# Ten additions of weight halves on GpSimd in place of VectorE, in a recurrence and mixture-of-experts kernel

## The chip, the cores and the metric

The kernel runs on one core of one Trainium2 chip. The metric is the device time of one execution in microseconds (us); lower is better. Engines are called by their short names: PE is TensorE (matmuls; PEld is its weight load), DVE is VectorE, ACT is ScalarE, POOL is GpSimd, SP issues most of the DMAs.

## What is computed

Two blocks follow each other, all in float32. The first is a recurrence over 768 time steps, for 4 batches of 8 heads of width 40:

```python
for t in range(S):
    y[:, :, t] = einsum('bhd,bhde->bhe', rt, state)
    Sa = einsum('bhde,bhe->bhd', state, at)
    state_decay = state * wt[:, :, None, :] - einsum('bhd,bhe->bhde', Sa, bt)
    state = state_decay + einsum('bhd,bhe->bhde', vt, kt)
```

Its output, laid out as x of 3072 tokens by 320, goes into a mixture of four experts, all of which see every token (w1 is 320x1024 and w2 is 1024x320 for each expert):

```python
p = domain_probs / (domain_probs.sum(-1, keepdims=True) + 1e-09)
for e in range(E):
    h = maximum(x @ w1[e], 0.0)
    out += p[:, e:e + 1] * (h @ w2[e])
```

## The kernel before

**Units.** The recurrence is cut into chunks of 64 time steps. A unit is one chunk of two batches; there are 24, numbered 0 to 23, and two of them make up one chunk of all four batches. Within a unit the recurrence becomes matmuls on 64x64 blocks and one triangular solve. `within` prepares a unit (decays G, the turned operands AT, RT and VT, the scaled n_tok and k_tok, score matrices F, ET and VC). `substitute` does the solve: copies of F's diagonal blocks into `blocks` (two on DVE, two on ACT), one large transpose into M on DVE, a few products on DVE, and then 16 rounds of a product (L585) and two additions (L598) of small tiles Z. For units 0 and 1 the rounds run on DVE, for all others on POOL. `merge` turns Z into Qc and QTc (DVE) and QT (four copies on POOL, L617), and joins the two halves of the solve through the matmuls pY and pQ. `step` is the part that depends on the state: RH (DVE), SN (ACT), psat, SaT and SX, pxr, RS, pdy, then the output Y and the new state.

**The mixture.** Work of the experts is a list of pieces, `todo`, from which `gap` takes one or two at four places in every unit, so that PE has work while the recurrence waits. For units 0 and 1 it is done plainly (`mixture_of_unit`). From the second chunk on, `mixture_of_chunk` does the second matmul for two units together by a Strassen-like scheme on halves: of the hidden values (`add_h`, L903, on DVE) and of the second weights (`add_weights`, L869). The latter makes, for each expert, three new tiles in `sums` and overwrites two halves of `w2_sb` in place: five operations of 128x640, made once, before the first `down_1` of their expert; expert 2's are read first at unit 5's `gap(1)`, expert 3's in the same unit's `gap(3)`. The tile of `sums` of the last expert is before that the place of the constant `pick`, which the matmuls pxT of units 0 to 3 read; the other three hold pieces of the first weights up to unit 1's mixture.

**Where the sums stand.** `sums_at` says how many of them are issued at which `gap`: one at each from unit 2's `gap(1)` to unit 4's `gap(2)`, which is experts 0 and 1, and then 2, 3, 2 and 3 at the four gaps from unit 4's `gap(3)` to unit 5's `gap(2)`, which is experts 2 and 3.

**Order.** A planner orders each engine's instructions by priority and its own estimate of when their inputs are there. `tc.keep_in_program_order` pins an instruction behind the one written just before it on the same engine. Matmuls of the main loop are pinned, as are the sums, the solve's first operations and the copies on POOL. The loop over u runs the step of unit u, the merge and the first part of the step of unit u + 1, and the preparation and the solve of unit u + 2. At the head of an iteration POOL has just been given the solve of unit u + 1; the QT copies of unit u + 1 and the solve of unit u + 2 follow. Units below `EARLY` (5) have a different order of these parts from later ones.

Of the kernel before, what the change touches and what calls it, by code (L numbers as in the profile page):

```python
# [15 lines left out]
def kernel(  # L16
# [38 lines left out]
    nc = tc.nc  # L55

    B, H, S, D = r.shape
    E, DM, F = moe_w1.shape
# [26 lines left out]
    def big(name):  # L85
# [6 lines left out]
        out=ident[:], in_=ident[:], pattern=[[1, P]], compare_op=ALU.is_equal, fill=0.0,  # L92
# [5 lines left out]
    for t, n, op in ((upf, L, ALU.is_gt), (diagf, Q, ALU.is_equal)):  # L98
        nc.vector.memset(t[:], 1.0)
        for q in range(P // n):  # L100
            o = slice(q * n, (q + 1) * n)
            nc.gpsimd.affine_select(
                out=t[o], in_=t[o], pattern=[[1, n]], compare_op=op, fill=0.0, base=0, channel_multiplier=-1,
# [83 lines left out]
    def sooner(wanted):  # L187
        return tc.high_priority(offset=SOONER) if wanted else nullcontext()
# [3 lines left out]
    def begin(u):  # L192
        q = Unit()
        q.u, q.c, q.bp = u, u // (B // 2), u % (B // 2)
        q.b = [2 * q.bp, 2 * q.bp + 1]
        q.start, q.end = q.c == 0, q.c == NC - 1
        q.apart = u >= EARLY + 2
        q.n = {}
        units.append(q)
        return q  # L200

    def load(q, names):
        for x in names:
            q.n[x] = t = sb.tile([P, H, D], FP32, name=f"nat{x}", tag=f"nat{x}", bufs=2 if x in "WV" else 1)
            for i, bb in enumerate(q.b):
                nc.sync.dma_start(
                    out=t[i * L:(i + 1) * L], in_=srcs[x][bb, :, q.c * L:(q.c + 1) * L, :].rearrange("h t e -> t h e"),
                )
# [30 lines left out]
    def go(moves, eng=None):  # L239
        for move in moves:  # L240
            move(eng or nc.sync)
# [362 lines left out]
    def merge(q):  # L604


        Qc = sb.tile([P, H, Q], FP32, name="Qc", tag="q", bufs=2)
        QTc = sb.tile([P, H, Q], FP32, name="QTc", tag="q", bufs=2)
        tc.keep_in_program_order(nc.vector.transpose(out=dealt(Qc[:]), in_=q.Z))
        tc.keep_in_program_order(  # L610
            nc.vector.transpose(  # L611
                out=QTc[:].rearrange("p h r -> p (h r)"), in_=Qc[:].rearrange("p h c -> p (h c)"),
            )
        )
        q.QT = QTs()
        for i in range(P // Q):
            ins = nc.gpsimd.tensor_copy(out=q.QT[quarter(i), :, quarter(i % 2)], in_=QTc[quarter(i)])  # L617
            tc.keep_in_program_order(ins)
        yield

        def two_heads(name, lhsT, rhs, to):
            p = big(name)
            for n in range(NJ):
                for r in range(2):
                    matmul(
                        out=p[half(r), n * 2 * Q:(n + 1) * 2 * Q], lhsT=lhsT[half(r), 2 * n:2 * n + 2, :],
                        rhs=rhs[half(r), 2 * n:2 * n + 2, :], start=True, stop=True,
                    )
            for r in range(2):
                for y in range(2):  # L630
                    src = p[quarter(2 * r + y), 0:H * Q].rearrange("p (n two t) -> p n two t", two=2, t=Q)[:, :, y, :]
                    with sooner(name == "pY"):
                        nc.scalar.copy(out=of_slot(to[quarter(2 * r)], y), in_=src)

        Y = Ys()
        two_heads("pY", q.below, QTc, Y)
        yield

        two_heads("pQ", Qc, Y, q.QT[:, :, quarter(1)])
        yield  # L640
# [212 lines left out]
    def of_w2(e, q, x):  # L853
        return w2_sb[e][:, q * HF:(q + 1) * HF, x * HD:(x + 1) * HD]

    def of_sums(e, n):
        return sums[e][:, n * HF * HD:(n + 1) * HF * HD].rearrange("p (f d) -> p f d", d=HD)

    def add_weights(e):

        b = {(q, x): of_w2(e, q, x) for q in range(2) for x in range(2)}
        for to, x, y, op in (
            (of_sums(e, 0), b[0, 0], b[1, 1], ALU.add),
            (of_sums(e, 1), b[0, 0], b[0, 1], ALU.add),
            (of_sums(e, 2), b[1, 0], b[1, 1], ALU.add),
            (b[0, 1], b[0, 1], b[1, 1], ALU.subtract),
            (b[1, 0], b[1, 0], b[0, 0], ALU.subtract),
        ):
            tc.keep_in_program_order(nc.vector.tensor_tensor(out=to, in0=x, in1=y, op=op))  # L869
            yield  # L870

    def mixture_of_chunk(qs, xT):
# [98 lines left out]
    def begin_later(n):  # L971
        for move in later[:n]:
            tc.keep_in_program_order(move(nc.sync))
        del later[:n]

    def mix(n):

        for piece in todo[:n]:
            ready = stores[:]
            del stores[:]  # L980
            piece()
            for begin_store in ready:
                begin_store()
            begin_later(3 if n > 1 else 6)
        del todo[:n]

    def lead():
        if todo and hasattr(todo[0], "lead"):
            todo[0].lead()

    def run(gen, n=99):
        if gen is None:
            return
        for _ in range(n):
            if next(gen, gen) is gen:
                break
# [3 lines left out]
    def begin_step(u):  # L1000
        q = units[u]
        if q.bp == 0:
            chunks_x[q.c] = sb.tile([P, 3, 2 * P], FP32, name="xT", tag="xT", bufs=2)
        q.xT = chunks_x[q.c][:, :, q.bp * P:(q.bp + 1) * P]
        return step(q, q.xT)
# [95 lines left out]
    sparse = range(4 * 1, 4 * 4 + 2)  # L1101

    sums_at = {4 * 2 + n: 1 for n in range(1, 11)}
    sums_at.update({4 * 4 + 3: 2, 4 * 5 + 0: 3, 4 * 5 + 1: 2, 4 * 5 + 2: 3})
    sum_ops = (None for e in range(E) for _ in add_weights(e))
    for u in range(1, NU):
        in_order[0] = True
        q = units[u]
        m = s_next = w = w_next = iter(())
        if u + 1 < NU:  # L1110
            m, s_next = merge(units[u + 1]), begin_step(u + 1)
            w_next = ws[u + 1]
        if u + 2 < NU:
            w = ws[u + 2]

        def gap(n, pieces=None):
            at = 4 * u + n
            run(sum_ops, sums_at.get(at, 0))
            mix((1 if at in sparse else 2) if pieces is None else pieces)

        early = u < EARLY
        if early:
            begin_later(len(later))
        ahead = u + 3 < NU and u in range(EARLY, EARLY + 3)
        if ahead:
            go(load_raw(begin(u + 3), "W"))
        if early:
            lead()
        run(w_next, 99 if early else 1)
        run(s, 1)  # L1130
        gap(0)


        if early:
            run(s, 1)
        run(w, 1)
        if not early:
            run(w_next)
            run(s)

        if early:
            run(w, 1)
            gap(1, 2 if u + 1 == EARLY else None)
            run(s)
        if u == 1:
            mixture_of_unit(q)
        elif q.bp:
            mixture_of_chunk(units[u - 1:u + 1], chunks_x[q.c])
        if not early:
            begin_later(len(later))  # L1150
            run(w, 1)
            lead()
            todo[:2] = todo[1::-1]
            gap(1)
            run(m, 1)

        if u + 3 < NU:
            go(load_raw(units[u + 3] if ahead else begin(u + 3), "A" if ahead else "WA"))
            load(units[u + 3], "WBKV")
            later.extend(load_raw(units[u + 3], "VR"))  # L1160
        run(w, 2)

        soon = u in (2, 3, 4)
        if soon:
            run(w, 1)
        if early:
            run(m, 1)
        else:
            run(m, 1)
            run(s_next, 1)  # L1170
            lead()
            run(m, 1)
            if u + 3 < NU:
                ws.append(within(units[u + 3]))
                run(ws[u + 3], 1)
        if soon:
            substitute(units[u + 2], nc.gpsimd)
        gap(2)

        if u == 1:  # L1180
            run(s_next, 1)
            run(m, 1)
        if not soon:
            run(w, 1)
        if not soon and u + 2 < NU:
            with sooner(not early):
                substitute(units[u + 2], nc.gpsimd)
        if not early:
            lead()
            run(s_next, 1)  # L1190
        if early:
            run(w, 1)
        if early:
            ws.append(within(units[u + 3]))
            run(ws[u + 3], 1)
            if u > 1:
                run(m, 1)
                run(s_next, 1)
            run(m)
            gap(3, 1)  # L1200
            run(s_next, 1)
        else:
            begin_later(len(later))
            gap(3)
        s = s_next
# [31 lines left out]
```

## Time and profile before

| | us |
|---|---|
| median of 3 runs | 1095.37 (1095.02 to 1099.68) |
| the profiled execution's own time | 1096.91 |
| its span in the profile | 1095.2 |
| PE busy | 1068.1 (98%) |
| DVE busy | 759.0 (69%) |
| POOL busy | 490.3 (45%) |
| the 20 sums on DVE (L869): 12 into sums, 8 in place | 10.4 and 6.8 |
| mean of one of them | 0.88 and 0.87 |

The profile is one execution, taken by the hardware profiler. In a group of instructions the columns are line, engine, operation, tiles written and read, shape and count, then busy time and mean duration in ns. In a timeline they are the start and the duration in us and what ran; in brackets stands the idle time of the engine just before, and what ended it. Most operations on PE go through a helper, so they all have line L76; there the names of the tiles tell them apart. Durations on POOL are rougher than those of other engines. The solves of units 4, 5, 6 and 7 on POOL begin at 149.5, 179.8, 212.2 and 264.1 us.

### The profile page before, as it was taken

The numbers are of one execution on the slowest core, as the hardware profiler recorded it, in microseconds if no ns is written. First come the engines' busy times: TensorE is split into PE (matmuls) and PEld (weight loads), VectorE is DVE, ScalarE is ACT, GpSimd is POOL, SyncE is SP. The second block draws the span as 40 slices with busy tenths as digits, with TensorE's granted clock in tenths as the row PEclk, the third lists the DMA queues.
The fourth block names the chain that finished last, engine by engine and source line by source line (L and its number), as shares of the span: only waits on it lengthen the run. The fifth ranks groups of instructions, "written<-read, shape, count | busy, mean of one in ns | idle before, by whom it ended". The sixth has DMA issues, their size and how long they took to land.

```text
span 1095.2 us, 38536 instructions
## 1 busy us (share of the span) xinstructions
PE 1068.1 (98%) x16102; PEld 959.0 (88%) x16102; DVE 759.0 (69%) x1551; ACT 353.4 (32%) x956; POOL 490.3 (45%) x1274
## 2 busy tenths in 40 slices
PE   7798999999999999999999999999999999999998
PEld 6677788889998999999999999989999999998887
DVE  7676569887776777767768768767777676544343
ACT  2432444234223333333233242343333332221110
POOL 5206577763472562653643634735625536420000
PEclk8799999999999999999999999999999999999999
DMA  7876545434444463454454454444543532322320
GB/s 118 236 231 142 131 91 131 107 77 108 120 119 105 110 144 97 103 146 97 100 133 105 106 122 106 115 99 105 131 103 85 149 89 60 99 71 79 107 75 13
DMA packets 268869, 122.19 MB, mean 112 GB/s; under 512 B 213736, under 2 KB 242072, under 8 KB 268696
## 3 DMA queue, kind: packets, MB, share of 16 engines
q1 hardware_dynamic: 265416, 119.12, 43.4%
q8 instruction: 127, 2.08, 0.8%
q10 hardware_dynamic: 3280, 0.61, 0.4%
q14 instruction: 46, 0.38, 0.1%
HBM read 111.79 MB, written 3.93 MB: 106 GB/s over the span
## 4 chain that ended last, share of the span: by engine, by line
PE 92%; DVE 4%; ACT 1%; DMA 1%; issue 1%; SPq 0%; DVEq 0%; ACTq 0%
PE ph L76 39%; PE p L76 31%; PE pdy L76 3%; PE psat L76 2%; PE pxr L76 2%; PE po L76 2%; PE prn L76 2%; PE pfe L76 1%; PE pc L76 1%; PE pQ L76 1%; PE pev L76 1%; PE pg L79 1%; PE pY L76 1%; DVE Z L595 1%; PE pe L76 1%
## 5 line engine op out<-in xcount | busy, mean ns | idle before, releaser
L76 PE MATMUL ph<-xT,w1p 128*128 128x256 f32 (+3 forms) x3040 | 443.9, 375 | 3.7 <-issue 3.6
L76 PEld LDWEIGHTS ph<-xT,w1p 64*64 64x64 f32 (+1 forms) x3040 | 337.7, 162 | 59.3 <-issue 18.9
L598 POOL TENSOR_TENSOR Z<-Z 128x31 f32<-128x31 f32 (+7 forms) x704 | 254.8, 362 | 55.2
L903 DVE TENSOR_TENSOR a<-hs 128x512 f32<-128x512 f32 x220 | 153.3, 714 | 105.9 <-ACT hs L784 105.9
L784 ACT ACTIVATE hs<-ph 128x512 f32<-128x512 f32 (+1 forms) x208 | 117.1, 564 | 332.0 <-PE ph L76 331.7
L585 POOL TENSOR_TENSOR Z<-M,Z 128x62 f32<-128x62 f32 (+7 forms) x352 | 148.6, 422 | 99.0 <-DVE M L574 73.1
L76 PE MATMUL p<-sums,a 128*128 128x160 f32 x1056 | 164.9, 299 | 0.0
L76 PEld LDWEIGHTS p<-sums,a 128*128 128x128 f32 x1056 | 152.8, 190 | 2.2
L797 DVE SCALAR_TENSOR_TENSOR osb<-p,gate,osb 128x320 f32<-128x320 f32 (+1 forms) x243 | 108.0, 481 | 62.6 <-PE p L76 57.5
L555 POOL COPY below<-F 32x256 f32<-32x256 f32 x48 | 21.4, 446 | 232.2 <-ACT F L511 230.6
L76 PEld LDWEIGHTS p<-w,hs 128*128 128x128 f32 x704 | 98.6, 190 | 8.5 <-issue 7.3
L76 PE MATMUL p<-w,hs 128*128 128x160 f32 x704 | 104.9, 302 | 0.0
L76 PE MATMUL p<-w,a 128*128 128x160 f32 x704 | 102.8, 299 | 0.0
L76 PEld LDWEIGHTS p<-w,a 128*128 128x128 f32 x704 | 98.0, 190 | 0.0
L617 POOL COPY QT<-QTc 32x256 f32<-32x256 f32 x96 | 40.4, 421 | 81.9 <-DVE QTc L611 68.7
L706 ACT COPY RS<-pxr 64x256 f32<-64x256 f32 x88 | 32.2, 366 | 99.7 <-DVE SX L404 66.6
L540 ACT COPY EV<-pev 64x160 f32<-64x160 f32 x96 | 23.0, 286 | 91.6 <-PE pev L76 91.2
L455 DVE RECIPROCAL gp<-gp 128x320 f32<-128x320 f32 x24 | 51.6, 2151 | 0.7
L404 DVE COPY_PREDICATED VC<-mask_up,pc 128x256 f32<-128x256 int32 x48 | 18.7, 442 | 45.4 <-PE pc L76 45.3
L558 DVE STREAM_TRANSPOSE M<-blocks 128x1024 f32<-128x1024 f32 x24 | 47.2, 1969 | 2.9 <-ACT blocks L552 2.4
L511 ACT COPY F<-pfe 128x256 f32<-128x256 f32 x48 | 15.5, 376 | 80.9 <-PE pfe L76 79.3
L76 PE MATMUL pdy<-VC,k_tok 64*64 64x104 f32 (+1 forms) x768 | 38.2, 259 | 0.0
(149 smaller groups left out, 1343.9 us busy)
## 6 DMA issues: line engine op xcount, KB each, us to landing
w1p<-in_moe_w_dram SPq DMA_DIRECT2D x95, 512.0 KB
w1p<-in_moe_w_dram SPq DMA_DIRECT2D x190, 64.0 KB
w<-in_moe_w_dram SPq DMA_DIRECT2D x4, 1280.0 KB
sums<-in_moe_w_dram SPq DMA_DIRECT2D x9, 512.0 KB
natW<-in_w_dram SPq DMA_DIRECT2D x48, 80.0 KB
natB<-in_b_dram SPq DMA_DIRECT2D x48, 80.0 KB
natK<-in_k_dram SPq DMA_DIRECT2D x48, 80.0 KB
out_dram<-osb SPq DMA_DIRECT2D x46, 80.0 KB
```

Of the source, the lines that this page charges most:

```text
L76: return stated(nc.tensor.matmul(**k))
L455: pin(nc.vector.reciprocal(out=gp[:], in_=gp[:]))
L540: nc.scalar.copy(out=of_slot(q.EV[half(p)], i ^ p)[:, :, 0:D], in_=pev[i][half(p)])
L555: tc.keep_in_program_order(nc.gpsimd.tensor_copy(out=q.below[quarter(i)], in_=q.F[quarter(i), :, 0:Q]))
L558: ins = nc.vector.transpose(out=M[:], in_=cols)
L585: ins = eng.tensor_tensor(out=Z[:, 1:3, 0:n, j + 1:Q], in0=M[:, j:j + 2, None, j + 1:Q].to_broadcast([P, 2, n, m]), in1=Z[:, here, 0:n, j: ...
L598: eng.tensor_tensor(out=z[:, 0], in0=z[:, 0], in1=z[:, x], op=ALU.add)
L617: ins = nc.gpsimd.tensor_copy(out=q.QT[quarter(i), :, quarter(i % 2)], in_=QTc[quarter(i)])
L706: nc.scalar.copy(out=RS[half(s), x ^ s::2], in_=prs[x][half(s)].rearrange("p (j i) t -> p j i t", i=2),)
L784: nc.scalar.activation(out=h[:, i * HF // 2:(i + 1) * HF // 2, 0:n], in_=ph[i][:], func=ACTF.Relu,)
L797: nc.vector.scalar_tensor_tensor(out=to, in0=p, scalar=sc, in1=to, op0=ALU.mult, op1=ALU.add)
L903: nc.vector.tensor_tensor(out=t[:], in0=x, in1=y, op=op)
```

## The change

The five operations of each of experts 2 and 3 are issued on POOL, those of experts 0 and 1 stay on DVE where they were. The ten are issued at the heads of iterations: three of expert 2 at unit 3's (the new tiles), two at unit 4's (the halves in place), and all five of expert 3 at unit 5's. On POOL that is after the solve of units 4, 5 and 6 in turn and ahead of that unit's QT copies.

```diff
     def add_weights(e):
 
+        eng = nc.vector if e < 2 else nc.gpsimd
         b = {(q, x): of_w2(e, q, x) for q in range(2) for x in range(2)}
...
-            tc.keep_in_program_order(nc.vector.tensor_tensor(out=to, in0=x, in1=y, op=op))
+            tc.keep_in_program_order(eng.tensor_tensor(out=to, in0=x, in1=y, op=op))
             yield
...
     sums_at = {4 * 2 + n: 1 for n in range(1, 11)}
-    sums_at.update({4 * 4 + 3: 2, 4 * 5 + 0: 3, 4 * 5 + 1: 2, 4 * 5 + 2: 3})
-    sum_ops = (None for e in range(E) for _ in add_weights(e))
+    sum_ops = (None for e in range(2) for _ in add_weights(e))
+    sums_at_head = {3: 3, 4: 2, 5: 5}
+    more_sums = (None for e in range(2, E) for _ in add_weights(e))
     for u in range(1, NU):
...
             run(sum_ops, sums_at.get(at, 0))
             mix((1 if at in sparse else 2) if pieces is None else pieces)
 
+        run(more_sums, sums_at_head.get(u, 0))
         early = u < EARLY
```

## The prediction

> **What bounds the kernel now.** I read the busy shares first, then the stretches around the moved work, then each engine's timeline there. In the first fence the columns after the engine's name are busy time, share of the span, count; in the stretches they are length, then busy time (and count) of PE, PEld, DVE, ACT, POOL, then clock, DMA share and GB/s.
>
> ```profile
> PE 1068.1 (98%) x16102; PEld 959.0 (88%) x16102; DVE 759.0 (69%) x1551; ACT 353.4 (32%) x956; POOL 490.3 (45%) x1274
> ```
> ```profile
> 173.00:185.00 12.00, 11.87 (x197) 9.45 (x192) 11.85 (x24) 5.92 (x18) 7.42 (x15) 1.00 0.49 117
> 205.00:212.00 7.00, 5.70 (x54) 4.98 (x46) 6.92 (x15) 1.45 (x4) 2.75 (x7) 1.00 0.57 140
> 212.00:239.00 27.00, 26.42 (x464) 23.04 (x456) 22.01 (x40) 9.83 (x29) 23.00 (x48) 1.00 0.46 104
> 239.00:248.00 9.00, 9.00 (x163) 8.35 (x165) 8.89 (x22) 3.12 (x8) 2.64 (x4) 1.00 0.07 16
> ```
>
> TensorE is the bound and its order is pinned, so only a new hole in PE costs time and only an old hole can be won. VectorE is a mere 69% busy overall, but full in three of these four stretches (11.85 of 12, 6.92 of 7, 8.89 of 9 us): a delay handed to it there is passed on. The three stretches are those right after the solves of units 4, 5 and 6, which end at 172.63, 204.75 and 238.88 by GpSimd's timeline (start, duration, what):
>
> ```profile
> 172.11 0.52 POOL L598 TENSOR_TENSOR Z<-Z 128x8 f32<-128x8 f32 x2
> 174.22 1.73 POOL L617 COPY QT<-QTc 32x256 f32<-32x256 f32 x4 [1.59 <-DVE QTc L611]
> ...
> 204.24 0.51 POOL L598 TENSOR_TENSOR Z<-Z 128x8 f32<-128x8 f32 x2
> 206.19 1.73 POOL L617 COPY QT<-QTc 32x256 f32<-32x256 f32 x4 [1.43 <-DVE QTc L611]
> ...
> 238.37 0.51 POOL L598 TENSOR_TENSOR Z<-Z 128x8 f32<-128x8 f32 x2
> 245.00 2.80 POOL L617 COPY QT<-QTc 32x256 f32<-32x256 f32 x4 [6.12 <-PE ph L76]
> ```
>
> Each sum is pinned behind GpSimd's previous instruction, so three sums land at 172.6, two at 204.8 and five at 238.9, always between a solve's last addition and the QT copies. The reader sees gaps of 1.6, 1.4 and 6.1 us there.
>
> [...] GpSimd's one 128x512 product (AT, at 43.24) took 1.525 us, and a VectorE two-input operation ran until 43.63; the remaining 1.13 us over 512 is 2.2 ns. [...] VectorE's state product stretches by up to 0.3 us beside solves whose operations take about that long. That a 1.4 us GpSimd operation blocks VectorE for as long, no run here shows yet. [...] VectorE's copies of 256 and 128 elements took 284 and 224 ns, 0.47 ns an element, against (777-650)/128 = 1.0 for additions[...].
>
> ```profile
> L732 DVE TENSOR_TENSOR state<-state,gl x44: 307/370/607, 46.1 to 922.7; 128x160 f32<-128x160 f32 x44
> L485 POOL TENSOR_TENSOR AT<-AT,G x1: 1525/1525/1525, 43.2 to 43.2; 128x512 f32<-128x512 f32 x1
> ```
>
> **The change part by part.**
>
> *Removed.* Ten VectorE additions of 128x640. They ran at 218.38 to 220.2 (two), 226.38 to 229.1 (three), 245.39 to 247.1 (two) and 250.98 to 253.3 (three), 8.7 us by the mean of 0.875 us. What PE could win is its holes nearby: 0.15 us at 218.1 (waits for ACT's Yq) and 0.42 us at 224.5 (waits for ACT's SX). Neither is VectorE's, so I book a gain of 0.4 us at most, from shorter VectorE queues. GpSimd's solve of unit 6 gains too: it stretched to 26.7 us (212.21 to 238.88) against 21.6 for the next one; without the five sums beside it I expect it 2.3 us shorter. That is off PE's path.
>
> *Added.* Ten GpSimd operations. [...] 640 x 2.2 = 1.41 us; with about 0.1 us between starts, 1.5 us each: 4.5, 3.0 and 7.5 us in the three gaps. No DMA is added or moved. Waits on weights and on the tiles' earlier readers are long over (the last pxT, which reads sums, ran at 170), and the results are wanted by PE only at about 238 (expert 2) and past 258 (expert 3). I cost those at nothing. Queued behind the sums on GpSimd are the QT copies, the below copies, Z's start and the next solve; VectorE's Qc and ACT wait on these only through the solve.
>
> *Gap A, three sums, 172.7 to about 177.4.* VectorE's two block copies [...] meet sums 2 and 3. Copy one waits for sum 2's end at 175.6, sum 3 slips in ahead of copy two, and copy two runs at 177.4 to 177.7. M's transpose then starts at about 178.0, not 175.57: 2.4 us late. VectorE has no idle time until 185, so RH moves from 182.31 to 184.7; behind it hang ACT's SN and QT copies (182.66 to 184.27) and PE's psat at 184.6, with 0.25 us to spare. New PE hole: 2.1 us. The QT copies end at about 179.2, 5 us before psat: covered. The solve of unit 5 starts at 182.2, not 179.79, since M is late.
>
> *Gap B, two sums.* In PE's time (shifted by A) the solve ends 0.3 us later than before[...]. The block copies at 206.29 lose between 0.4 and 1.6 us, as they fall before or after the second sum. VectorE is full to 211, and PE's hole of 1.30 us at 210.26 ends when VectorE's second read of p75 (211.08, 0.38 us) frees its bank. That hole grows by the same amount; I take the middle, 1.0 us.
>
> *Gap C, five sums.* If the solve ends 2.3 us sooner, at 236.6, the first two sums run under VectorE's reciprocal (one input, 237.26 to 239.4), free. The other three stand in a stretch with five two-input VectorE operations: Y*G at 240.17 (0.68 us), two state products (0.32 us each), n_tok and k_tok (0.48 us each). Y*G waits for sum 3 (to 241.1), the first state product for sum 4 (to 243.2), n_tok for sum 5 (to 244.9), k_tok ends at about 246.0, not 242.35. Then VectorE's four evictions, Qc, QTc and RT come 3.6 us late. PE's pNT at 244.75 loses 0.65 us, pKT 0.3 more, and pc at 245.72, which reads RT (ready at 245.46 before), loses altogether about 3.4. If the solve ends no sooner, all five sums alternate with these operations and PE loses near 6; if VectorE's operations go first, near 0. I take 3.3 us.
>
> **Sum:** 2.1 + 1.0 + 3.3 - 0.4 = 6.0 us. The profiled execution's own time was 1096.91 us around a span of 1095.2; the median of the runs is 1095.37, 1.5 us lower. I put the 6.0 us on the median: 1101.4 us.
>
> **Rivals.**
> 1. [...] The largest stretch of VectorE seen is 0.3 us; if GpSimd gives way between parts of a long operation, or VectorE's queued operation is served first, each of about ten conflicts costs no more than 0.3 us: 3 us over all, a third of it absorbed, less the 0.4 us gain: about +1.6, 1097.0 us. This decides once VectorE's lateness stays under about 1 us in each gap. For it: four VectorE additions of 0.715 us at 185.42 ran with GpSimd beside them and hardly slowed. Against: GpSimd's operations were a few tenths long there.
> 2. *GpSimd's own queue turns late.* If blocked sums take 2.5 us instead of 1.5, gap A fills to 180.2, QT, below and Z's start take 3.0 us more, and the solve of unit 5 starts at 183.2: 1.3 us late even in PE's shifted time. VectorE then waits in Qc ahead of the p75 read: about 1.3 us more in B, and the fuller price in C (6 rather than 3.3): about 10 us in all, 1105.4 us. For it: solves already swell from 21.6 to 26.7 us by conflict. Against: GpSimd is idle for 10.76 us before the next below copies at 258.57.
> 3. *Faster through a lighter VectorE.* It would need holes in PE that VectorE's sums cause; those near them add to 0.57 us: 1094.8 us. More needs a luckier order of the whole queue.
>
> **How the numbers follow.** The forecast has 0.55, with its own range 1099.4 to 1104.4 (A 1.0 to 2.4, B 0.4 to 1.6, C 2 to 5); rival 2 has 0.16, rival 1 has 0.26, rival 3 has 0.03. 0.5% is 5.5 us, about what a measurement of this kernel can tell from no change; it lies at 1100.85. About two thirds of the forecast's cases (0.36) and all of rival 2 lie above: slower 0.52. Rival 1 and the remaining third of the forecast: same 0.45. Faster by as much: 0.03. The range that leaves out no more than 2 in 10 runs from 1094.5, below rival 1 and rival 3's middle, to 1106.5, past rival 2's middle.
>
> **What would show it.** Sums on GpSimd at about 1.5 us each, starting within 0.2 us of a solve's end; VectorE's block copies after the unit-4 solve taking over 2 us together, not 0.88; new PE holes of about 2 us before psat, about 2.3 us (1.3 before) in ph before the p75 read, and some 3 us spread over pNT, pKT and pc near 245 to 250. It is wrong if VectorE's block copies and n_tok keep their lengths (rival 1), if Qc waits for Z (rival 2), or if PE's extra idle time lies elsewhere, which would mean that the order of the queues has changed.

## Result and profile after

The kernel with the ten sums on GpSimd took 1105.68 us (median of 6 runs, 1104.09 to 1107.61). The kernel before, run beside it, took 1097.05 us (6 runs, 1094.26 to 1099.68). The ratio is 1.008 with a 95% interval of 1.0058 to 1.0103: **slower, by 8.6 us**. The profiled execution took 1106.2 us around a span of 1104.5. Line numbers behind the change are one higher than before: the sums are L870, `add_h`'s additions L904.

The page's busy shares, columns as for the kernel before:

```profile
PE 1071.8 (97%) x16102; PEld 961.1 (87%) x16102; DVE 755.4 (68%) x1541; ACT 354.1 (32%) x956; POOL 505.8 (46%) x1284
```

VectorE has ten instructions less, yet only 3.6 us less busy time, though those ten had taken 8.7 us: the other 5 us came back as longer instructions. The stretches around the three solves' ends, moved with the work (length, then PE, PEld, DVE, ACT, POOL, clock, DMA share, GB/s), show where PE is short of work:

```profile
173.00:185.00 12.00, 11.11 (x158) 8.78 (x150) 11.88 (x21) 4.14 (x13) 9.73 (x15) 1.00 0.44 110
208.00:215.00 7.00, 4.89 (x39) 4.26 (x41) 6.96 (x12) 0.93 (x3) 4.48 (x9) 1.00 0.50 108
215.00:239.00 24.00, 23.42 (x370) 20.21 (x363) 12.99 (x29) 9.39 (x28) 20.07 (x49) 0.93 0.46 109
239.00:253.00 14.00, 11.87 (x167) 10.65 (x168) 13.32 (x23) 2.62 (x5) 9.79 (x8) 1.00 0.08 18
```

VectorE is full where PE idles most (11.88 of 12, 6.96 of 7, 13.32 of 14 us). PE's waits between 165 and 262 us (who waited for whom: us in total, times, longest), after:

```profile
PE pc L76 <- DVE RT L245: 2.1, 1, 2.1
PE ph L76 <- issue: 2.1, 1, 2.1
PE pxr L76 <- issue: 1.4, 1, 1.4
PE psat L76 <- ACT QT L633: 1.0, 2, 0.8
```

and the same question put to the kernel before, where pc and psat don't appear at all:

```profile
PE ph L76 <- issue: 1.3, 1, 1.3
...
PE pxr L76 <- issue: 0.4, 1, 0.4
```

GpSimd's timeline after (start, duration, what). The sums stand where the prediction put them, straight behind a solve's last additions:

```profile
172.07 4.62 POOL L870 TENSOR_TENSOR sums<-w 128x640 f32<-128x640 f32 x3
176.63 1.80 POOL L617 COPY QT<-QTc 32x256 f32<-32x256 f32 x4
...
206.63 3.07 POOL L870 TENSOR_TENSOR w<-w 128x640 f32<-128x640 f32 x2
...
238.93 5.46 POOL L870 TENSOR_TENSOR sums<-w 128x640 f32<-128x640 f32 x3
244.34 3.50 POOL L870 TENSOR_TENSOR w<-w 128x640 f32<-128x640 f32 x2
251.93 1.74 POOL L617 COPY QT<-QTc 32x256 f32<-32x256 f32 x4 [4.09 <-DVE QTc L611]
```

VectorE's timeline at the same places:

```profile
173.82 3.01 DVE L552 COPY blocks<-F 32x256 f32<-32x256 f32 x2
...
208.52 1.72 DVE L552 COPY blocks<-F 32x256 f32<-32x256 f32 x2
...
214.12 0.38 DVE L797 SCALAR_TENSOR_TENSOR osb<-p,minus_gate,osb 128x160 f32<-128x160 f32 x1
...
245.11 1.33 DVE L726 TENSOR_TENSOR Y<-Y,G 128x512 f32<-128x512 f32 x1
246.36 1.66 DVE L732 TENSOR_TENSOR state<-state,gl 128x160 f32<-128x160 f32 x1
...
248.18 0.48 DVE L476 SCALAR_TENSOR_TENSOR n_tok<-natB,gp 128x320 f32<-128x320 f32 x1
...
251.72 0.67 DVE L245 STREAM_TRANSPOSE RT<-rawR 128x512 f32<-128x512 f32 x1
```

The same instructions before:

```profile
174.31 0.88 DVE L552 COPY blocks<-F 32x256 f32<-32x256 f32 x2
...
206.29 0.88 DVE L552 COPY blocks<-F 32x256 f32<-32x256 f32 x2
...
240.17 0.68 DVE L726 TENSOR_TENSOR Y<-Y,G 128x512 f32<-128x512 f32 x1
240.77 0.32 DVE L732 TENSOR_TENSOR state<-state,gl 128x160 f32<-128x160 f32 x1
```

The two pairs of block copies, Y*G and the state product are where the prediction looked for blocking; n_tok, which it also named, kept its 0.48 us.

**PE's lateness, matmul by matmul.** Taking the same matmul in both traces and the difference of its start times (after less before): -0.5 us at 154, +1.25 within psat, +2.2 at the end of the pxr wait, +3.0 where PE waits for VectorE's read of p75 (ph at 214.60, 0.1 us behind that read's end), +4.7 some 4 us later, +6.8 at pc, +8.4 at 256. (Lateness is more than idle time: psat loses 1.8 us, of which the list of waits shows 1.0.) Two of these steps, 3.0 to 4.7 and 6.8 to 8.4, are no holes. They are stretches in which PE was busy at half clock, as three windows of the profile after show (column seven is the clock):

```profile
99.00:112.00 13.00, 11.19 (x129) 9.45 (x127) 8.33 (x13) 2.66 (x6) 10.38 (x30) 1.00 0.59 152
210.00:220.00 10.00, 7.89 (x43) 6.05 (x42) 9.79 (x20) 0.60 (x1) 6.68 (x15) 0.83 0.62 113
246.00:258.00 12.00, 9.87 (x171) 8.91 (x170) 9.28 (x22) 4.24 (x12) 3.42 (x5) 0.86 0.18 57
```

The same of the kernel before:

```profile
99.00:112.00 13.00, 11.20 (x121) 9.68 (x120) 8.22 (x12) 2.31 (x6) 9.61 (x29) 0.87 0.66 152
210.00:220.00 10.00, 8.54 (x137) 6.96 (x136) 9.79 (x20) 3.70 (x12) 6.93 (x12) 1.00 0.59 105
246.00:258.00 12.00, 12.00 (x227) 11.09 (x221) 11.29 (x23) 4.55 (x15) 1.71 (x3) 1.00 0.42 103
```

The clock records give each stretch exactly: 3.41 us at 0.5, which costs 1.7 us. After the start of the kernel, after has two, at 215.7 and 253.2; before has one, at 106.9.

### The profile page after: what moved, and what is told of

It reads as the page before. It is cut to its first block, busy times and chain, and to the rows that moved or that the text cites. A ratio compares the mean times of both kernels' runs of the same rounds, so it can differ in the third digit from the quotient of the medians.

```text
span 1104.5 us, 38540 instructions
## 1 busy us (share of the span) xinstructions
PE 1071.8 (97%) x16102; PEld 961.1 (87%) x16102; DVE 755.4 (68%) x1541; ACT 354.1 (32%) x956; POOL 505.8 (46%) x1284
## 4 chain that ended last, share of the span: by engine, by line
PE 88%; DVE 5%; issue 1%; ACT 1%; DMA 0%; DVEq 0%; SPq 0%
PE ph L76 38%; PE p L76 30%; PE pdy L76 3%; PE psat L76 2%; PE po L76 2%; PE pxr L76 2%; PE prn L76 2%; PE pc L76 1%; PE pfe L76 1%; PE pev L76 1%; PE pQ L76 1%; PE pe L76 1%; PE pY L76 1%; PE pg L79 1%; PE pNT L79 1%
## 5 line engine op out<-in xcount | busy, mean ns | idle before, releaser
L598 POOL TENSOR_TENSOR Z<-Z 128x31 f32<-128x31 f32 (+7 forms) x704 | 259.2, 368 | 55.2
L904 DVE TENSOR_TENSOR a<-hs 128x512 f32<-128x512 f32 x220 | 151.8, 707 | 113.4 <-ACT hs L784 113.4
L585 POOL TENSOR_TENSOR Z<-M,Z 128x62 f32<-128x62 f32 (+7 forms) x352 | 143.0, 406 | 98.0 <-DVE M L574 72.1
```

What stands on the lines that cost most here:

```text
L585: ins = eng.tensor_tensor(out=Z[:, 1:3, 0:n, j + 1:Q], in0=M[:, j:j + 2, None, j + 1:Q].to_broadcast([P, 2, n, m]), in1=Z[:, here, 0:n, j: ...
L598: eng.tensor_tensor(out=z[:, 0], in0=z[:, 0], in1=z[:, x], op=ALU.add)
L904: nc.vector.tensor_tensor(out=t[:], in0=x, in1=y, op=op)
```

## Experiments

The theory: while a long GpSimd instruction runs, VectorE's operations with two inputs in SBUF and its copies within SBUF wait for it (in after two copies took 3.01 us in place of 0.88, a state product 1.66 in place of 0.32), and VectorE hands the delay to PE at psat, p75 and pc. The rivals: GpSimd's queue is late by itself (the queue theory of the expectations); VectorE's relief counts; the half clock, not the wait, is what costs. All ratios are against the kernel before, run in the same series (medians 1098.2, 1098.26 and 1097.94 us). A loss in us is the ratio's, times that median; the difference of the medians can lie up to 1.8 us off it. Traces are one execution each, so a hole of one trace need not be in every run.

**One gap at a time.** only3 moves only expert 2's three new tiles to GpSimd (gap A); only5 moves only expert 3's five sums (gap C). The others are on VectorE at gaps of `sums_at` (in only3 expert 2's last two one gap earlier than before).

```diff
 only3, in add_weights
-        eng = nc.vector if e < 2 else nc.gpsimd
...
+            eng = nc.gpsimd if e == 2 and n < 3 else nc.vector
 and sums_at_head = {3: 3}
 only5
-        eng = nc.vector if e < 2 else nc.gpsimd
+        eng = nc.vector if e < 3 else nc.gpsimd
 and sums_at_head = {5: 5}
```

> Only expert 2's first three sums are on GpSimd, at the head of unit 3; the other seven stay on VectorE at the gaps they had. [...] the two block copies after the solve of unit 4 take about 3.0 us together against 0.88 in the kernel before, psat and pxr come 2.7 us late, no halved clock follows, and the time is 2.5 to 3.5 us over the kernel before. Queue theory (what costs is that GpSimd itself comes late to the QT copies and the next solve): the copies on VectorE keep their 0.9 us, the solve of unit 5 starts about 1.3 us late, and the time is within 1.5 us of the kernel before.

only3: 1100.06 us, ratio 1.0024 (1.0012 to 1.0035), +2.6 us. One group of VectorE's timeline and two of PE's waits in its trace:

```profile
172.85 2.99 DVE L552 COPY blocks<-F 32x256 f32<-32x256 f32 x2
```
```profile
PE pxr L76 <- issue: 1.4, 1, 1.4
PE psat L76 <- ACT QT L633: 0.9, 2, 0.8
```

The block copies lose the same 2.1 us as in after, and psat waits. The pxr wait of 1.4 us (0.4 before) comes with it although no sum stands there. There was no half clock in this area.

> Only expert 3's five sums are on GpSimd, at the head of unit 5; expert 2's five stay on VectorE. [...] of VectorE's operations beside the sums, Y times G and the state products stretch by 2 to 3 us together, pc waits for RT with a hole of about 2 us; if the hole halves TensorE's clock for one stretch of 3.4 us, 1.7 us more: 2 to 4 us over the kernel before. Queue theory: the QT copies come late, but psat reads them 10 us later: no change, within 1 us.

only5: 1105.07 us, ratio 1.0066 (1.0047 to 1.0086), +7.2 us, where 2 to 4 were expected. VectorE's timeline and PE's waits:

```profile
241.89 1.59 DVE L726 TENSOR_TENSOR Y<-Y,G 128x512 f32<-128x512 f32 x1
243.40 1.66 DVE L732 TENSOR_TENSOR state<-state,gl 128x160 f32<-128x160 f32 x1
244.99 0.31 DVE L731 TENSOR_TENSOR state<-pdy,state 128x160 f32<-128x160 f32 x1
245.22 1.59 DVE L476 SCALAR_TENSOR_TENSOR n_tok<-natB,gp 128x320 f32<-128x320 f32 x1
246.74 1.66 DVE L732 TENSOR_TENSOR state<-state,gl 128x160 f32<-128x160 f32 x1
```
```profile
PE pc L76 <- DVE RT L245: 2.5, 1, 2.5
...
PE pKT L79 <- DVE k_tok L481: 1.3, 1, 1.3
```

Alone, gap C is worse than inside the whole change: four VectorE operations are blocked instead of two, (1.59 - 0.68) + 2 x (1.66 - 0.32) + (1.59 - 0.48) = 4.7 us. In after, VectorE comes to this stretch 4 us later against the sums (its reciprocal starts at 242.2, 3.3 us behind the first sum), so three of the five sums are over by the time that Y*G comes; in only5 the reciprocal starts at 238.98, before the first sum at 239.87. PE's holes at pNT, pKT and pc add to 4.1 us. A half-clock stretch of 6.8 us from 250.1 adds about 2.2 by PE's lateness (6.3 us at pc, 8.6 at 257), since PE idles in part of it.

Some 2.4 us of PE's lateness in this trace come before gap C: a p75 hole of 2.1 us, 0.8 more than before, and a half clock at 212.6. There VectorE's Qc had waited for the end of GpSimd's solve of unit 5, though no sum stands in front of it:

```profile
205.33 0.63 DVE L609 STREAM_TRANSPOSE Qc<-Z 128x256 f32<-128x256 f32 x1 [0.71 <-POOL Z L598]
```

**Sums or mere presence.** fills leaves all sums on VectorE and gives GpSimd, at the three places, constant fills of the same length, which only write. Its edit is against the kernel before.

```diff
-    sums_at.update({4 * 4 + 3: 2, 4 * 5 + 0: 3, 4 * 5 + 1: 2, 4 * 5 + 2: 3})
+    sums_at.update({4 * 4 + 3: 2, 4 * 5 + 0: 3, 4 * 5 + 2: 5})
...
+        for _ in range({3: 3, 4: 2, 5: 5}.get(u, 0)):
+            tc.keep_in_program_order(nc.gpsimd.memset(sums[3 if u == 5 else 2][:, 0:1664], 0.0))
```

> All sums are on VectorE as in the kernel before (expert 3's five together at unit 5's gap 2), and GpSimd makes constant fills of 1664 elements, about 1.5 us each, that read nothing, at the three places: three, two and five. [...] the block copies after the solves of units 4 and 5 take about 3.0 and 1.7 us, while Y times G and the state products at unit 5's head keep their lengths: 3 to 6 us over the kernel before. If fills shut out both kinds: 8 to 9 us over. If GpSimd's queue alone matters: also 8 to 9 us over, with the copies at 0.9 us.

fills: 1103.08 us, ratio 1.0028 (1.0004 to 1.0053), +3.1 us (4.9 by the medians). VectorE's timeline, and GpSimd's fills at unit 5's head:

```profile
173.32 2.96 DVE L552 COPY blocks<-F 32x256 f32<-32x256 f32 x2
...
207.82 1.66 DVE L552 COPY blocks<-F 32x256 f32<-32x256 f32 x2
...
243.66 0.68 DVE L726 TENSOR_TENSOR Y<-Y,G 128x512 f32<-128x512 f32 x1
```
```profile
241.62 7.67 POOL L1122 MEMSET sums<- 128x1664 f32 x5
```

This parts the two kinds of conflict. Block copies were held up by a write-only fill as much as by a sum (2.96 us here, 2.99 in only3); Y*G (0.68), the state products (0.32) and n_tok (0.48) ran in the middle of five fills and were not touched. That they would not be was the author's estimate; no run had shown it before this one. GpSimd's queue has the same places and nearly the same lengths in fills as in after, so queue and length alone don't explain gap C.

**How long one instruction is.** split cuts each of the ten sums in four of 128x160, five_split does so for gap C alone.

```diff
-            tc.keep_in_program_order(eng.tensor_tensor(out=to, in0=x, in1=y, op=op))
+            for f in [slice(0, HF)] if e < 2 else [slice(f, f + 1) for f in range(HF)]:
+                tc.keep_in_program_order(eng.tensor_tensor(out=to[:, f], in0=x[:, f], in1=y[:, f], op=op))
 five_split: e < 3, and sums_at_head = {5: 5} as in only5
```

> The changed kernel with each GpSimd sum cut into four of 128x160: 40 instructions in place of 10 in the same three places, same bytes, 2 to 4 us more of GpSimd's time in all. [...] the block copies take at most 1.5 us together, TensorE's new holes stay under 1 us each, the clock is not halved after them, and the time is 1 to 4 us over the kernel before, 5 us under the changed one. Queue theory: GpSimd's queue is longer still, so as slow as the changed kernel or slower, 8 to 11 us over the kernel before.

split: 1103.06 us, ratio 1.0045 (1.0028 to 1.0062), +4.9 us, where 1 to 4 were expected. VectorE's block copies are back at 0.92 and 0.80 us, psat waits no more and pc only 0.9 us. GpSimd's own queue turned late: in gap A twelve pieces took 5.95 us instead of 4.62, the QT copies behind them 3.95 instead of 1.80, and the solve of unit 5 began at 185.87 instead of 181.44 (the last additions before the sums were 1.6 us later than in after). That solve still ended at 208.84, before VectorE's Qc was due at 210.33, so this lateness is not seen to reach PE. What PE lost most at in this trace is the longest pxr wait of all, 2.5 us, with a half clock after it at 193.2. So splitting all of them gained less than expected, and why pxr waits stays open.

> Expert 3's five sums alone on GpSimd at unit 5's head, each cut into four of 128x160; expert 2's on VectorE. GpSimd's queue has 10 us of slack behind them here. [...] no operation of VectorE's waits more than about 0.4 us, holes before pKT and pc together under 1.2 us in place of 3.9, no halved clock: 0 to 2 us over the kernel before, 5 to 7 us under the five whole sums. If the length of a hold does not matter but only GpSimd's total time: as slow as the five whole sums, 7 us over.

five_split: 1099.42 us, ratio **1.0007** (0.9996 to 1.0017), against 1.0066 for only5. Its groups of pieces (count, then ns least, median, most) and its wait at pc:

```profile
L871 POOL TENSOR_TENSOR sums<-w x12: 520/528/977, 239.6 to 246.0; 128x160 f32<-128x160 f32 x12
L871 POOL TENSOR_TENSOR w<-w x8: 521/522/532, 246.5 to 249.8; 128x160 f32<-128x160 f32 x8
```
```profile
PE pc L76 <- DVE RT L245: 1.2, 1, 1.2
```

The same work on the same engine at the same place, in pieces of 0.53 us instead of 1.55: GpSimd is busy longer (10.9 us against 8.4), and yet about 6 of only5's 7 us are gone. VectorE meets the sums as in only5: its reciprocal starts 0.9 us ahead of the first one in both traces. Y*G took 0.99, the state products 0.64, n_tok 0.58 and k_tok 0.81, 1.4 us lost against 4.7, and PE's holes here are 1.2 us against 4.1. What costs is how long one GpSimd instruction is.

**The copies elsewhere.** blocks_act gives the block copies of units 5 and 6 to ScalarE and keeps the change.

```diff
-            move = nc.scalar.copy if i >= 2 else nc.vector.tensor_copy
+            move = nc.scalar.copy if i >= 2 or q.u in (5, 6) else nc.vector.tensor_copy
```

> The changed kernel with the four block copies of units 5 and 6 all on ScalarE, none on VectorE. [...] nothing of VectorE's is shut out after the solves of units 4 and 5, so psat is late by less than 0.5 us, the p75 hole is back near 1.3 us and no half-speed stretch follows it; unit 5's head stays as it is (about 2 us and a half-speed stretch of 1.7 us): 3 to 5 us over the kernel before, 4 to 5 less than the changed one. Queue theory: TensorE's holes stay, since GpSimd's sums stand where they stood: the changed kernel's time.

blocks_act: 1104.31 us, ratio 1.0048 (1.0033 to 1.0062), +5.3 us, where 3 to 5 were expected. The psat hole is gone and pxr's is 0.6 us. At p75 nothing was won, since another two-input operation met the sums in the copies' place:

```profile
210.02 1.82 DVE L904 TENSOR_TENSOR a<-hs 128x512 f32<-128x512 f32 x1
```

PE's p75 hole was 2.6 us and pc's 2.5, and no half clock followed them. Freeing one victim helps only where no other stands behind it.

**The same sums where VectorE has slack.** in_idle issues expert 3's five sums behind unit 6's QT copies; expert 2's are on VectorE.

```diff
-        run(more_sums, sums_at_head.get(u, 0))
...
+            if u == 5:
+                run(more_sums, 5)
```

> Only expert 3's five sums are on GpSimd, behind unit 6's QT copies, where GpSimd then idles over 10 us; expert 2's are on VectorE as before. [...] VectorE has there the scan and four additions of hidden halves, which may each wait up to 1.5 us, and TensorE waits for those additions: 0 to 2 us over the kernel before, no half-speed stretch. Queue theory: GpSimd has nothing to do there, so no loss and perhaps 0.5 us of gain. A VectorE freed of 4 us could gain at most 1 us.

in_idle: 1098.15 us, ratio 0.9997 (0.9987 to 1.0008). GpSimd's and VectorE's timelines:

```profile
245.73 4.55 POOL L870 TENSOR_TENSOR sums<-w 128x640 f32<-128x640 f32 x3
250.25 4.49 POOL L870 TENSOR_TENSOR w<-w 128x640 f32<-128x640 f32 x2
```
```profile
248.98 2.38 DVE L443 TENSOR_TENSOR_SCAN G<-G,first 128x512 f32<-128x512 f32 x1
251.40 1.34 DVE L447 TENSOR_TENSOR gl<-gl,G 128x8 f32<-128x8 f32 x1
```

VectorE is blocked here as well: the scan takes 1.23 us and the tiny product 0.17 where no sum stands. But PE doesn't wait for either, and the time does not move. The blocking is not the cost; what waits behind it is.

**Is there anything to win?** none leaves the ten sums out on both engines.

```diff
+    nc.gpsimd.memset(sums[2][:, PIECE:], 0.0)
+    nc.gpsimd.memset(sums[3][:], 0.0)
...
-        run(more_sums, sums_at_head.get(u, 0))
```

> The ten sums of experts 2 and 3 are left out on both engines (their three tiles are cleared at the start instead), so the output is not the reference's. This prices what VectorE's lighter load is worth with nothing put on GpSimd. My working held it to 0.4 us at most, as TensorE's holes nearby are not VectorE's: within 0.1% of the kernel before. If VectorE's 8.7 us had been on the path: 3 to 8 us under it.

none: 1099.06 us, ratio 1.0008 (0.9995 to 1.002). Taking ten sums off VectorE, with nothing put on GpSimd, gains nothing.

**The half clock.** warm_hole puts two dummy matmuls into the p75 hole, warm_both also four ahead of pc, both on top of the change; five_warm puts two ahead of pKT and five ahead of pc on top of only5.

```diff
 warm_hole, at the p75 piece
+        for _ in range(2 if k == 20 else 0):
+            matmul(out=ph[0][half(0), 0, :], lhsT=w1.last[part(0), 0, half(0)], rhs=xT[part(0), 2, :], start=True, stop=True)
 warm_both, five_warm: dummies of ident by ident into the bank of pc (and pKT), as
+                matmul(out=p[0][half(0), 0:P], lhsT=ident[half(0), half(0)], rhs=ident[half(0), :], start=True, stop=True)
```

> The changed kernel with two dummy matmuls [...] into the first of the two banks, just ahead of the matmul that waits for VectorE's read of p75 in unit 4; their result is overwritten. TensorE's hole of 2.1 us there is filled with work, at no cost in order. If it is the hole that halves the clock: no half-speed stretch near 215, and 1.5 us less than the changed kernel. If the halved clock comes from elsewhere (the chip's load at this time): it stays, and the time is the changed kernel's.

> The same, and four dummy matmuls of 128 columns [...] ahead of pc in unit 5, where TensorE waits 2.1 us for RT. If holes halve the clock: no half-speed stretch near 215 nor near 253, 3 us less than the changed kernel, about 5 us over the kernel before, which is what the holes themselves cost. Otherwise the changed kernel's time.

> Expert 3's five whole sums on GpSimd at unit 5's head, and dummy matmuls of 128 columns [...] in the holes that they make: two ahead of pKT, five ahead of pc, into banks that are overwritten next. The holes' length stays 3.9 us, but TensorE is not idle in them. If holes halve the clock: no half-speed stretches near 250 (6.8 us long before, worth 3.4 us), and 2.5 to 3.5 us less than the five whole sums without dummies, 3.5 to 5 us over the kernel before. If the clock has another cause: no change, 7 us over.

None did what was expected of its time. warm_hole: 1108.35 us, ratio 1.0081 (1.0055 to 1.0106). warm_both: 1110.33, 1.0099 (1.0069 to 1.0128). five_warm: 1109.71, 1.0109 (1.0086 to 1.0131). In warm_hole PE's p75 hole was down to 1.0 us, the half clock at 215 did vanish, and PE, 1.0 us behind after's at 190, was 1.0 us ahead of it at 231; it then waited 2.5 us at pc, because RT's time is set by GpSimd's sums and VectorE, which had not moved, and the half clock at 253.2 came as in after. In warm_both both stretches are gone, but one follows a pxr hole of 1.9 us at 191.5, and one comes at 358.8. In five_warm half of the pKT and pc holes was filled (0.6 and 1.2 us of waiting were left of 1.3 and 2.5), and the half clock of 6.8 us still came (251.8); why, the runs don't show. All three also waited longer than the others for ph between 265 and 400 us: 3.4, 5.0 and 4.8 us, against 1.7 in after and at most 2.7 in any other run. Whether the added matmuls cause that, these runs don't tell.

The mean granted clock of all runs answers the rival better than single traces do. It was 0.988 in blocks_act and 0.988 in the kernel before of its series, so hardly any of that run's 5.3 us can be the clock's; fills had 0.988 too. It was 0.986 in after and in only5, against 0.988 before (in only5's series). By an estimate from the shares of all runs that is some 5 us more at half clock, so 2 to 3 of their 7 to 9 us, give or take as much. In five_warm it was 0.983, so the dummies did not raise it.

## Why the prediction was right

Forecast 1101.4 us, range 1094.5 to 1106.5, slower by over 0.5% at 0.52: it came out slower by 0.8%, inside the range, near its upper end. (The base that it started from, 1095.37 us of three runs, was 1.7 us under the 1097.05 measured beside the change.) Of the 8.6 us, 6.0 had been worked out; the rest is in two terms that the sum hadn't got, with one term too large. PE's new holes came to 5.6 us, and that this is so near 6.0 is in part luck: gap C was put 1.2 us too large, and pxr's 0.9 us was left out. By its own steps:

- **Price of a sum: right.** Forecast 1.5 us each; the least were 1.53, gaps A and B took 4.62 and 3.07 us; gap C took 8.9 instead of 7.5, since sums waited for VectorE there. The least of 640 and of 160 elements (1.53 and 0.52 us) give 2.1 ns an element, against 2.2. That a 1.4 us GpSimd operation blocks VectorE's copies and two-input operations for about as long was the author's estimate, which no run had shown; it is now shown (3.01 for 0.88 us of copies; 1.66 for 0.32).
- **Gap A: right in place, 0.6 us too small.** The copies ended at 176.8, M's transpose started at 177.2, the solve of unit 5 at 181.44 (forecast 182.2), QT came in time. psat came 1.8 us late (forecast 2.1). What was missing is the pxr wait behind it, 0.9 us more. With it A is 2.7 us; only3 alone gave 2.6.
- **Gap B: right in after's trace, not isolated.** Forecast +1.0 (0.4 to 1.6); the hole went from 1.30 to 2.11 us, +0.8, which is what the copies lost (1.72 for 0.88). No run moves gap B's sums alone, and only5 has a hole of the same 2.1 us without them, so one trace proves little here.
- **Gap C: right mechanism, smaller hole than forecast.** 3.3 us were forecast with three operations blocked; in after it was two, 0.65 + 1.34 = 2.0 us, and a hole of 2.1. The solve of unit 6 did get shorter (215.25 to 238.98, 23.7 us, against 26.7), by 3.0 rather than 2.3, but the forecast had the first sum start 0.7 us ahead of the reciprocal. In after it started 3.3 us ahead, so three sums were over before Y*G; in only5 0.9 us behind. How VectorE and GpSimd meet decides this term, as only5 shows with 4.1 us of holes for the same five sums.
- **Relief: nothing,** where 0.4 at most was booked (none, 1.0008).
- **Missing term: the half clock,** 2 x 1.7 us in the profile after. The sum counted a hole at its length and put what comes behind it at nothing. Not all of it is the change's: the profile before had one such stretch at 106.9, which after had not, and five_split and none had one at 213.0 and 214.6 with hardly any loss against before. The one behind pc's hole appears only with the sums in gap C (after, only5, warm_hole, five_warm). Psat 1.8, pxr 0.9, p75 0.8, pc 2.1 and the half clock's 3.4 add to 9.0 us, against the 8.9 by which PE's lateness grew from -0.5 to +8.4.

Rival 1 (a stretch of 0.3 us at most) fell: one conflict costs up to 1.34 us. Rival 2's 1105.4 us is nearer to the result than the forecast, but its mechanism did not happen in after: GpSimd's QT copies had ended 6 us ahead of psat, and Qc did not wait for Z. In split GpSimd's queue did turn late, and Qc did not wait there either; only in only5 did unit 5's Qc wait for over 0.2 us, with no sum in front of it. Rival 3 fell by none.

**The parts need not add up:** only3's +2.6 and only5's +7.2 make 9.8 without gap B, against 8.6 for the whole; the intervals are too wide to call that a difference. The traces show why it may be one: at p75 and pc PE waits for a chain of GpSimd and VectorE, so lateness that PE has collected before can be taken up in the next hole. In warm_hole the time won at 215 was lost at pc.

**Open:** the pxr wait. It is 1.2 to 2.5 us in the six traces with sums or fills in gap A and block copies on VectorE (after, only3, fills, split, warm_hole, warm_both), and at most 0.6 in the other seven. In the traces a 16 KB transfer of the instruction queue lands 1.2 to 1.6 us ahead of its end (189.03 for 190.29 in after, 188.1 for 189.37 in only3, 190.28 for 191.74 in split; 186.51 for 188.06 with a wait of only 0.42 before), so PE may be waiting for instructions; this was read, not tried. Open too are the waits of ph past 265 us.

## What to carry to other kernels

Before giving GpSimd an elementwise operation, lay its length beside VectorE's timeline. Here VectorE's operations with two inputs in SBUF that met a sum of 1.55 us were held up by as much as 1.34 us (a state product, 1.66 for 0.32 us), and two fp32 copies within SBUF by 2.1 us together (2.99 for 0.88 in only3); only the slack behind those, not the busy shares, said what that cost. The same sums cost 7.2 us in one place and nothing a few us later; in quarters, where GpSimd had room, they cost about 1 us even in the bad place. Two operations were spared beside whole sums in only5: the reciprocal, with one input, kept its 2.15 us, and the sum of the matmul result pdy, in PSUM, and the state (L731), at 244.99, kept its 0.31 us while two sums ran from 244.84 to 248.21. And an engine that was 69% busy gave nothing back when it was relieved of ten sums (none, 1.0008): the bound engine did not wait for it there.

## What was not expected of the hardware

- **Holes of about 2 us were often followed by a half clock.** In the traces of before and after, all half-clock stretches but the last, which the kernel's end cuts off, are 3.413 us long or, at the start, 20.48, six times that; and within a trace they begin whole multiples of 3.413 us apart (after: 21.12, 215.68 and 253.23, which are 57 and 11 of them). With PE's idle time counted in steps of that length, the step ahead of the half clock held 2.11 and 2.13 us in after (215.68 and 253.23) and 1.80 in before (106.94). But a step with 1.81 us in after, from 103.04, was followed by the full clock, so idle time alone does not decide it; nor does the length of a hole, since no half clock followed those of 2.6 and 2.5 us in blocks_act, whose mean clock over all runs was the 0.988 of the kernel before. A half-clock stretch costs 1.7 us if PE is busy in it (lateness of 3.0 to 4.7 at 215.7 in after). So one and the same hole may cost its length or 1.7 us more.
- **A tiny operation was blocked as long as a large one:** a product of 128x8 took 1.34 us instead of 0.17 (in_idle).
- **GpSimd's sums wait as well:** 1.55 us undisturbed, 2.46 next to VectorE's scan and 2.07 next to its additions in in_idle.
